# A gated mix of a diagonal state-space layer and linear attention: complex states packed as 64 real and 64 imaginary rows

## The chip, the cores and the metric

The kernel runs on one core of a Trainium2 chip. The core has a matrix engine (PE, TensorE), a vector engine (DVE), an activation engine (ACT, ScalarE), a general engine (POOL, GpSimd) and a queue engine (SP, SyncE). PE reads its operands from the on-chip memory SBUF and writes to PSUM, eight banks of 512 float32 per partition; ACT or DVE must carry a result from PSUM back to SBUF, which is called an evacuation below. Transfers are issued from the queues of SP, ACT and POOL and run on 16 DMA engines. The metric is the device time of one execution in microseconds (us).

## What is computed

```python
g = sigmoid((x * gate_w).sum(-1, keepdims=True))
# a: a diagonal complex recurrence over 2048 steps, 512 states
Lam_bar = exp(dt * Lam);  B_bar = ((Lam_bar - 1) / Lam)[:, None] * (B_re + 1j * B_im)
h[t] = Lam_bar * h[t-1] + B_bar @ x[t]
a = 2 * (h @ C.T).real + x * Dskip
# b: attention without a score matrix, 32 heads of 16
q, k, v = split(x @ wqkv)
phi(u) = concat(softmax(u @ w_phi), softmax(-(u @ w_phi)))
b = (phi(q) @ (phi(k).T @ v)) / (phi(q) @ phi(k).sum(0) + 1e-6) @ wo
out = g * a + (1 - g) * b
```

x has 2048 rows of 512 in bfloat16. The gate g is one number per row.

## The kernel before

The rows of x are taken as 8 residues modulo 8 of 256 steps each, and lie in `xT` transposed, two tiles of 128 rows per residue; there are 16 tiles in all. The recurrence runs over the 256 steps of residue 7 only, with Lam_bar to the eighth, and the other residues follow from it by products with Lam_bar, its square or its fourth power. The 512 states are four groups j of 128.

The program is recorded stage by stage. A stage is a generator, `st_...`, each of whose steps records a few instructions. The table `ORDER` names the steps one after the other; `@` gives the PSUM banks a step takes and `:D` sends its evacuation or scaling to DVE rather than ACT. On every engine the instructions run in that order, each after what it depends on.

- `W`, `T`, `f`: transposes on PE of parts of the weights and of the first two tiles of x, and the product of the key weights with `w_phi`. `Z` are products of zeros ahead of them.
- `k`, `v`, `q`: the key, value and query products of one tile, four matmuls each. `x`, `n`, `e`, `s` (and `X`, `N`, `E`, `S` for queries) are the softmax features: trees of max and min, differences, exponentials and sums, on DVE and ACT, for two or four tiles together. `a` sums phi(k).T @ v in two PSUM banks and, with four matmuls of one column per tile, the gate's sum (L631).
- `V`, `P`, `U`, `M`, `M2`, `D`: from Lambda and dt the factors of the states, by small operations; `D` lays them out as diagonal 128 x 128 matrices `dg` (L437). `i` makes tables of cosines and sines.
- `b`: the product of B with one pair of residues (L641). `g`: the product for the next residue (L653), plus the states before it turned by Lam_bar (L660, L661), then by its square (L668, L669) and fourth power (L674, L675), all summed in PSUM. A complex turn takes, for each of the real and the imaginary result, two matmuls with diagonals. For j 2 and 3 the first turn is made by scalings and accumulating transfers instead (`l`).
- `z`: the scan over 256 steps (L723) with the tables' turns before and after it. `H`, `h`, `p` turn its result into the states of the other residues. They scale by the real part and by the imaginary part on ACT or DVE (L444, L446), and add by DVE (L839 to L843) or by accumulating transfers from POOL's queue (`add_by_dma`, L529). The sets `ZD`, `HD`, `HJ`, `PJ` say for which j a transfer adds.
- `c`: C times the factor of B_bar, in `C2`. `y`: the output products of a tile, eight matmuls with states and C2 (L875) and, for 12 of the 16 tiles, four with the diagonal of Dskip (L882); for the four tiles of `XD` DVE adds the Dskip term (L913, L947). `o`: the attention result (L894) and its normalization. `O`: its transpose by DMA; `t`: the product with `wo` into the same bank as `y` (L943), and the evacuation with the gate. `R` stores.

On SP's queue stand the loads, first the key weights and two tiles of x, then the DMA transposes of x in pairs of tiles (L232), with those of B (L238) and C among them, and from the middle on the transposes of the features and of `on`, and the stores.

Of the kernel before, what the change touches and what calls it, by code (L numbers as in the profile page):

```python
# [10 lines left out]
ALU = mybir.AluOpType  # L11
# [9 lines left out]
P = 128  # L21
# [15 lines left out]
q1@0 H0 z1 v7@1 q1 X0 s3 q7@7 q7 z1 s4 N0 X0 v6@3 b300@0 N0 H0 b301@7 H0:D H0 N0 X0 v6 N0 s3 a2 v5 a2 c0 a2 v7 a2 X0
b301 s3 b300 q4@1 l3:D l3:D l3 c2 X0 N0 H1 H1:D H1:D q4 s4 q5@0 l3 q5 q6@7 g210@6 q6 X1 N1 h0:D H1:D E0 b211@0 X1 s4
E0 b210@7 X1 s3 b210 b311@1 b310@3 g211@2 s4 N1 S0 b211 N1 S0 s4 s4 l3:D X1 g311@7 N1 s4 g210 g210 b310 g211 g211 H1
g310@3 h0 h0 h0 g210 h1:D g211 g210 h1 b311 g211 g210 h0 g211 z2 z2 S0 z2 z2 z2 z2 g311 h1 g311 g311 h1 g310 g310 g310  # L40
S0 p00 v9@2 z2 g310 g310 g311 g311 v8@6 v15@1 S0 z2 z3 v10@7 p00 v12@3 v9 v8 S0 S0 v15 v11@6 z3 z2 z2 H2 v10 q11@2
p00:D z3 z3 z3 H2 a3 a3 H2 v12 z3 H2 H2 v11 h2 p10:D z3 z3 S0 z3 a3 a3 z3 p01 X1 h1 H3 q8@3 H3 H3 q10@6 q10 v14@7 h2
h2 H3 H3 v13@1 v13 p00:D S0 h2 q11 a4 v14 N1 q9@6 h2 q9 h3:D h3:D q12@1 a4 q8 h3 q12 X2 p10 E1 E1 a4 a4 Y S0 h3 h3 Y
X2 G q13@3 q13 G Y Y y1@1 y0@0 y0 N2 END p01 y0 o0@6 p00 p11 o0 S1 o1@4 o1 q15@2 o0 p10 p10 X2 y3@3 S0 y1 p11 S1 o0 X2
N2 q15 o1 S1 o2@6 o2 N2 o2 S1 S1 y3 N2 o1 p01 y3 p10 y2@2 S1 S1 o2 S1 O0 p30 p30 o3@4 o3 o3 y1 y2 X2 y2 q14@6 q14 N2
y6@7 o3 y6 t1 y7@6 G E2 E2 X3 N3 t0 y6 S1 X3 N3 G t0 X3 S1 o4@4 t1 y7 y7 o5@0 o4 o4 N3 O1 t2 X3 p01 N3 S2 S2 S2 o5 o5
t2 o4 S2 o5 S2 t3 t3 y4@4 S2 X3 S1 o6@0 S2 S2 o6 R0 o7@2 p20 y4 y4 o7 N3 p01 o6 o6 p20 o7 o7 y5@5 p30 E3 y5 O2 E3 y5
p20 S2 y8@0 t5 t4 p30:D y11@1 S2 R1 o9@2 p20 p20 p30 y8 t4 t5 o8@4 S3 p11:D p11 S3 S3 o8 S3 y11 o8 o8 o9 o9 o9 O3 t6
# [30 lines left out]
def kernel(  # L79
# [60 lines left out]

    aexp = nc.scalar.activation
# [6 lines left out]
    vec_n = const.tile([12, P], BF16, name="vec_n")  # L148
    vec_m = const.tile([8, P], BF16, name="vec_m")
# [3 lines left out]
    Wk2, Wv = WKV[:, 0, :, 0:DF], WKV[:, 1]  # L153
    C2 = const.tile([P, 2, PT, D], BF16, name="C2")
    warm = const.tile([P, D], BF16, name="warm")
    nc.vector.memset(warm[:], 0.0)
    nc.scalar.dma_start(out=Wc[:], in_=B_w_phi.rearrange("(k hl) e f -> (hl e) k f", hl=8))
# [98 lines left out]
    def xl(n):  # L256
        k = n - XD[0]
        return WKV[:, k // 4, k % 4, :]
# [764 lines left out]
```

## Time and profile before

| | |
|---|---|
| device time, median of 3 runs | 149.28 us (149.17, 149.65, 149.28) |
| the profiled execution | the page gives its span, 147.2 us, and no device time |
| PE busy | 140.8 us, 96% of the span, 1014 matmuls |
| DVE busy | 135.1 us, 92%, 330 instructions |
| ACT busy | 123.4 us, 84%, 222 instructions |
| POOL busy | 45.4 us, 31%, 61 instructions |
| DMA | 22.63 MB; SP's and ACT's queue q1 52.7% and POOL's q0 33.8% of 16 engines' time |

The span runs from the first to the last instruction. A row of a group reads: line, engine, operation, tiles written <- tiles read, shape, count | busy us, mean ns of one | idle time before, and what ended it. A row of waits reads: who waited <- for whom: us in total, times, longest. A row in order of time begins with its start and its length in us. `PS` is PSUM, `C`, `H` and `EE` are tiles whose number is left out. `C` in the first loads is a tile that holds the key weights and two tiles of x before it holds C2.

### The profile page before, as it was taken

To read this page: it belongs to the slowest core of one execution; us is meant where nothing else is said; L and a number is where in the kernel's file an instruction comes from. 1 tells how busy PE (TensorE), PEld (TensorE's weight loads), DVE (VectorE), ACT (ScalarE), POOL (GpSimd) and SP (SyncE) were. 2 spreads that over 40 slices of the span, in tenths; PEclk is the share of its full clock that TensorE was granted. 3 is DMA by queue.
4 is the path that set the end of the run, shared out by engine and by line. 5 is a ranking of instruction groups with operands and counts; after the bars stand their busy time and mean duration, and the time that the engine had idled before them with its cause. 6 is when DMAs were issued, how large, how long until landed. Compare 5 with 4: busy or idle time off the path is not lost.

```text
span 147.2 us, 2881 instructions
## 1 busy us (share of the span) xinstructions
PE 140.8 (96%) x1014; PEld 73.3 (50%) x1014; DVE 135.1 (92%) x330; ACT 123.4 (84%) x222; POOL 45.4 (31%) x61
## 2 busy tenths in 40 slices
PE   6999999999999999999999999999979999999990
PEld 2744444444544644554454656545445554545650
DVE  2879999999999999999999999999998999979740
ACT  3479999999999999999999999999988997912110
POOL 7503600003138195797545353051003003000000
PEclk9999999999999999999999999999999999999999
DMA  5999998990846586789878969969988999999643
GB/s 123 233 184 170 181 179 160 239 290 2 195 94 90 88 114 99 80 127 169 131 111 141 144 90 191 123 126 164 208 179 153 192 214 159 199 180 271 129 111 114
DMA packets 56047, 22.63 MB, mean 154 GB/s; under 512 B 44768, under 2 KB 54880, under 8 KB 56032
## 3 DMA queue, kind: packets, MB, share of 16 engines
q1 hardware_dynamic: 47584, 15.05, 52.7%
q0 software_dynamic: 7504, 7.09, 33.8%
q10 hardware_dynamic: 944, 0.31, 0.9%
q8 instruction: 8, 0.13, 0.4%
q14 instruction: 7, 0.06, 0.1%
HBM read 2.51 MB, written 2.10 MB: 31 GB/s over the span
## 4 chain that ended last, share of the span: by engine, by line
DVE 45%; PE 36%; ACT 9%; DMA 4%; issue 3%; DVEq 0%
PE PS L875 17%; PE PS L943 8%; DVE EE L597 6%; DVE mn L544 5%; DVE mx L544 5%; DMA phT<-EE 4%; DVE EE L555 4%; DVE sq L575 4%; DVE EE L561 3%; PE PS L894 3%; PE PS L493 3%; PE PS L324 2%; DVE w L723 2%; ACT vx L137 2%; ACT Xq L137 2%
## 5 line engine op out<-in xcount | busy, mean ns | idle before, releaser
L567 ACT ACTIVATE EE<-EE 128x2048 bf16<-128x2048 bf16 x16 | 30.3, 1933 | 0.4 <-DVE EE L561 0.4
L493 PE MATMUL PS<-WKV,xT 128*128 128x480 bf16 (+1 forms) x128 | 29.2, 372 | 0.2 <-ACT WKV L137 0.2
L493 PEld LDWEIGHTS <-xT 128*128 128x128 bf16 x192 | 18.1, 97 | 19.7 <-issue 0.9
L137 ACT CAST Xq<-PS 128x480 bf16<-128x480 f32 x32 | 17.5, 592 | 0.2
L653 PE MATMUL PS<-xT,BT 128*128 128x512 bf16 x64 | 16.2, 379 | 0.0
L875 PE MATMUL PS<-C,H 128*128 128x512 bf16 x64 | 15.6, 379 | 0.0
L943 PE MATMUL PS<-Wo,oT 128*128 128x512 bf16 (+2 forms) x68 | 15.5, 366 | 0.0
L493 PE MATMUL PS<-Wq,xT 128*128 128x480 bf16 x64 | 14.9, 365 | 0.0
L641 PE MATMUL PS<-xT,BT 128*128 128x512 bf16 x64 | 14.8, 379 | 0.0
L529 POOL DMA_DIRECT2D C<-CT x4 | 6.8, 1712 | 18.1 <-DVE CT L446 18.1
L907 DVE TENSOR_TENSOR on<-PS,rd 128x512 bf16<-128x512 f32 x16 | 10.9, 684 | 1.0 <-ACT rd L901 0.9
L529 POOL DMA_DIRECT2D eb<-dg x4 | 4.8, 1201 | 22.3 <-ACT dg L444 10.9
L949 ACT ACTIVATE ot<-PS,G 128x512 bf16<-128x512 f32 (+1 forms) x10 | 6.3, 647 | 4.7 <-PE PS L943 4.7
L641 PEld LDWEIGHTS <-BT 128*128 128x128 bf16 x64 | 6.3, 98 | 7.5
L561 DVE TENSOR_TENSOR EE<-mn,Xq 128x2048 bf16<-128x2048 bf16 (+1 forms) x9 | 9.9, 1095 | 0.0
L555 DVE TENSOR_TENSOR EE<-Xq,mx 128x2048 bf16<-128x2048 bf16 (+1 forms) x9 | 9.8, 1094 | 0.0
L575 DVE TENSOR_TENSOR sq<-EE 128x2048 bf16<-128x2048 bf16 (+1 forms) x9 | 9.8, 1094 | 0.0
L943 PEld LDWEIGHTS <-oT 128*128 128x128 bf16 x68 | 6.4, 98 | 6.7
L898 ACT ACTIVATE ld<-PS 128x32 f32<-128x32 f32 x16 | 3.0, 202 | 7.8 <-PE PS L894 7.8
L597 DVE TENSOR_TENSOR EE<-EE,rc 128x2048 bf16<-128x2048 bf16 x8 | 9.6, 1210 | 0.0
L653 PEld LDWEIGHTS <-BT 128*128 128x128 bf16 x64 | 6.1, 97 | 6.9 <-issue 0.2
L137 ACT CAST vx<-PS 128x512 bf16<-128x512 f32 x16 | 9.5, 618 | 0.0
(196 smaller groups left out, 329.7 us busy)
## 6 DMA issues: line engine op xcount, KB each, us to landing
out_dram<-ot SPq DMA_DIRECT2D x7, 256.0 KB, 2.5
C<-CT POOLq DMA_DIRECT2D x4, 256.0 KB, 5.2
eb<-CT POOLq DMA_DIRECT2D x4, 256.0 KB, 4.3
eb<-dg POOLq DMA_DIRECT2D x4, 256.0 KB, 4.3
sq<-sq POOLq DMA_DIRECT2D x3, 256.0 KB, 3.8
WKV<-in_B_wqkv_dram SPq DMA_DIRECT2D x1, 512.0 KB, 4.9
Wo<-in_B_wo_dram SPq DMA_DIRECT2D x1, 512.0 KB, 4.1
WKV<-in_A_x_dram SPq DMA_DIRECT2D x2, 256.0 KB, 4.8
```

The lines of the kernel that those rows point to most:

```text
L137: nc.scalar.copy(out=out_ap, in_=in_ap)
L493: MM(out=pt[:], lhsT=xT[:, kt, ti * P:(ti + 1) * P], rhs=W[:, kt, :], start=(kt == 0), stop=(kt == KT - 1))
L544: VT(out=dst, in0=cur[:, :, :, 0:n, :], in1=cur[:, :, :, n:2 * n, :], op=op)
L555: VT(out=half(EE, 0), in0=X5, in1=live["mx", p].to_broadcast([P, L, 8, Dh, 4]), op=ALU.subtract)
L561: VT(out=half(live["EE", p], 1), in0=live["mn", p].to_broadcast([P, L, 8, Dh, 4]), in1=X5, op=ALU.subtract)
L567: aexp(out=EE[:, l_:l_ + 2], in_=EE[:, l_:l_ + 2], func=ACT.Exp)
L575: VT(out=sq.rearrange("p q x i -> p x q i"), in0=e4[:, :, 0:2], in1=e4[:, :, 2:4], op=ALU.add)
L597: VT(out=E5[:, u:u + 2], in0=E5[:, u:u + 2], in1=rc[:, u:u + 2].to_broadcast([P, 2, 2 * NB, Dh, 4]), op=ALU.mult)
L641: MM(out=pb[:], lhsT=BT[:, ri, kt, j * P:(j + 1) * P], rhs=cells(kt, 2 * pr), start=(kt == 0), stop=(kt == KT - 1))
L653: MM(out=pgq[:], lhsT=BT[:, ri, kt, js], rhs=cells(kt, r1), start=(kt == 0), stop=(dst == 0 and j in LJ and kt == KT - 1))
L875: MM(out=py[:], lhsT=hs[j][ri], rhs=C2[:, 1 - ri, j, c:c + w], start=(j == 0 and ri == 0), stop=False)
L943: MM(out=py[:], lhsT=oT[:, g, :], rhs=Wo[:, g, c:c + w], start=False, stop=(g == HG - 1))
```

## The change

- The states of a group j are packed in another way: 64 states' real parts in partitions 0 to 63 and their imaginary parts in 64 to 127, in two halves q. A turn by a complex factor is then one matmul with a matrix of 2 x 2 blocks of diagonals, in place of two. All factors are made for 8 such groups of 64 (`CT2`), so the small operations have 8 columns, not 4.
- `g` has one matmul where two stood, and for all four j (`l` is gone). `H`, `h` and `p` go through PE too: one matmul per half (`spin4`) and a sum on DVE that reads PSUM; for four of the eight `p`, ACT evacuates and a transfer adds.
- `z` adds the sine product across the halves of the partitions, by two accumulating transfers of 64 partitions each (`swapped`), for all j. The tables are copied into the packed form by eight transfers (`tt`), C by eight (`cc`, into `Cp`).
- B is loaded by rows on SP's queue into `H1` (`Bn`, four loads) and transposed from there.
- The gate is a 481st column among the key weights, padded to 488, so `k` yields it and the 64 matmuls of one column go. `XD` is gone: `Dd` is used for all 16 tiles.
- Tiles of the pools are taken in rotation from fixed buffers (`rotating`), and the whole `ORDER` is another list.

On SP's queue, in the first loads, before (`C_68` is the tile of the key weights and x, `BT` B transposed):

```order
L223 DMA C_68<-in_B_wqkv_dram 128x512 x2
L228 DMA C_68<-in_A_x_dram 128x512 x2
L232 DMA_TRANSPOSE xT<-in_A_x_dram 128x4x256 x5
L238 DMA_TRANSPOSE BT<-in_A_B_re_dram 128x2x512
L232 DMA_TRANSPOSE xT<-in_A_x_dram 128x4x256
```

and now (`H_120` is `H1`):

```order
L240 DMA C_68<-in_B_wqkv_dram 128x512 x2
L245 DMA C_68<-in_A_x_dram 128x512 x2
L255 DMA H_120<-in_A_B_re_dram 64x4x512
L255 DMA H_120<-in_A_B_im_dram 64x4x512
L249 DMA_TRANSPOSE xT<-in_A_x_dram 128x4x256 x4
L261 DMA_TRANSPOSE BT<-H_120 128x8x128 x2
L249 DMA_TRANSPOSE xT<-in_A_x_dram 128x4x256 x2
```

Two loads of B moved ahead of all tiles of x, and the first transposes of B ahead of the fifth pair.

On PE, the turns that follow a product of `g`, before (weights of the diagonals `dg`, the states in `eb` and `H`):

```order
L660 LDWEIGHTS dg
L660 MATMUL PS<-eb_94,dg 128x512
L661 LDWEIGHTS dg
L661 MATMUL PS<-eb_94,dg 128x512
L668 LDWEIGHTS dg
L668 MATMUL PS<-H_117,dg 128x512
L669 LDWEIGHTS dg
L669 MATMUL PS<-H_117,dg 128x512
```

and now, with the last matmul of the product ahead of them:

```order
L691 LDWEIGHTS BT
L691 MATMUL PS<-xT,BT 128x512
L693 LDWEIGHTS dg
L693 MATMUL PS<-eb_98,dg 128x512
L699 LDWEIGHTS dg
L699 MATMUL PS<-H_120,dg 128x512
```

One matmul per turn is left of two. On DVE, where the sums of `H` and `h` stand among the features, before (`m` and `n` are the scaled states, `mx` the features' maxima):

```order
L797 TENSOR_TENSOR H_117<-m_1178,n_1179 128x512
L561 TENSOR_TENSOR EE<-mn,Xq 128x32x64
L799 TENSOR_TENSOR H_117<-m_1178,n_1179 128x512
L446 TENSOR_SCALAR m_1268<-H_116,dgs 128x1024
L446 TENSOR_SCALAR n_1269<-H_116,dgs 128x1024
L795 TENSOR_TENSOR m_1268<-m_1268,H_117 128x1024
```

and now:

```order
L753 TENSOR_TENSOR H_119<-PS,H_119 128x2x256
L586 TENSOR_TENSOR mx_338<-mx_338 128x32x8
L724 TENSOR_TENSOR mc_562<-vv_147,T_144 128x512
L727 TENSOR_TENSOR ms_573<-vv_147,T_144 128x512
L586 TENSOR_TENSOR mx_338<-mx_338 128x32x4
L768 TENSOR_TENSOR H_120<-PS,H_120 128x512 x2
```

The scalings are gone from there, and the sums take one operand from PSUM.

```diff
-B:D Lk Lk Z@0 Lx Z Z Z Z Z Z W00@1 Z B B B W01@2 W01 W01:D W00 W00 W10@0 Lx W11@3 Lx T0@4 B W11 T0 f1@2 Lx Lx f0@1 f0
...
+Z@7 Z Z Z Z Lk Lk W00@3 Z W01@4 W00 W00 Z Lx B:D B B B Lx Z W01 W01:D B T0@5 T0 T1@7 T1 W10@4 W11@1 f1@5 f1 V2@3 Bn Bn
...
+PA = ((0, 0), (0, 1), (1, 0), (1, 1))
-XD = (8, 9, 10, 11)
-LJ = (2, 3)
-ZD = (0, 1)
-HD = (0, 1)
-HJ = (0, 1)
-PJ = (0, 1)
...
+    def rotating(pool, bufs0):
+        slots = {}
+
+        def tile_of(shape, dtype, name, bufs=None):
+            s = slots.setdefault(name, [[], 0])
+            if not s[0]:
+                s[0] = [pool.tile(shape, dtype, name=f"{name}{k}", bufs=1) for k in range(bufs or bufs0)]
+            s[1] += 1
+            return s[0][(s[1] - 1) % len(s[0])]
+
+        return tile_of
...
+    nc.gpsimd.dma_start(out=vec_m[:], in_=gate_w.rearrange("(j p) -> j p", p=P))
     for n, src in enumerate((A_Lambda_im, A_Lambda_re, A_log_dt)):
-        nc.gpsimd.dma_start(out=vec_n[4 * n:4 * n + 4, :], in_=src.rearrange("(j p) -> j p", p=P))
+        nc.gpsimd.dma_start(out=vec_n[CT2 * n:CT2 * (n + 1), :].rearrange("c (d s) -> c d s", d=2),
+                            in_=src.rearrange("(c s) -> c s", s=P // 2).unsqueeze(1).to_broadcast([CT2, 2, P // 2]))
...
+    def st_Bn():
+        for h in range(2):
+            for ri, src in enumerate((A_B_re, A_B_im)):
+                nc.sync.dma_start(out=Bn0[64 * ri:64 * ri + 64, 4 * h:4 * h + 4, :],
+                                    in_=src[2 * h * P:2 * (h + 1) * P, :].rearrange("(c s) d -> s c d", s=64))
+                yield
+
     def st_Lb():
-        for ri, src in enumerate((A_B_re, A_B_im)):
-            for h in range(2):
-                trans(out=BT[:, ri, 2 * h:2 * h + 2, :], in_=src[:, 2 * h * P:2 * (h + 1) * P])
-                yield
+        for j in range(PT):
+            trans(out=BT[:, j].rearrange("p q k m -> p (q k) m"), in_=Bn0[:, 2 * j:2 * j + 2, :].rearrange("p q d -> p (q d)"))
+            yield
...
-            for kt in range(KT):
-                MM(out=live["acc"][1][:, 4 * KVW + ti:4 * KVW + ti + 1], lhsT=xT[:, kt, ti * P:(ti + 1) * P],
-                   rhs=gw_b[:, kt:kt + 1], start=False, stop=(n_ == NTI - 1 and kt == KT - 1), skip_group_check=True)
...
+        MM(out=pgq[:], lhsT=dg[:, 0, c, :], rhs=eb[j][:, q, dst], start=False, stop=(dst == 0))
...
-        MM(out=pgq[:], lhsT=dg[:, da, j, :], rhs=U1[:, 0, :], start=False, stop=False)
-        MM(out=pgq[:], lhsT=dg[:, db, j, :], rhs=U1[:, 1, :], start=False, stop=True)
+        MM(out=pgq[:], lhsT=dg[:, 1, c, :], rhs=U1[:, q, :], start=False, stop=True)
...
+    def swapped(out_ap, in_ap, b):
+        add_by_dma(out_ap[64 * b:64 * b + 64], in_ap[64 - 64 * b:P - 64 * b])
...
+    def spin4(j, k, out_ap, src, t=None):
+        for q in range(2):
+            pb = bank([P, N2], F32, "pb")
+            MM(out=pb[:], lhsT=dg[:, k, 2 * j + q, :], rhs=src[:, q], start=True, stop=True)
+            yield
+            if t is None:
+                VT(out=out_ap[:, q], in0=pb[:], in1=out_ap[:, q], op=ALU.add)
+            else:
+                evac(t[:, q], pb[:])
+            yield
+        if t is not None:
+            add_by_dma(out_ap, t)
+            yield
...
+    def st_cc(h):
+        for q in range(2):
+            for b in range(2):
+                nc.sync.dma_start(out=Cp[64 * b:64 * b + 64, 2 * h:2 * h + 2, q, :], in_=C2[64 * q:64 * q + 64, 1 - b, 2 * h:2 * h + 2, :])
+                yield
...
     def st_h(j):
...
+        yield from spin4(j, 1, H1[:, j], prevs(j))
...
+        yield from spin4(j, 0, eb[j][:, :, pr], src, CT[:, j] if (j, pr) in PA else None)
...
-        for kt in range(KT if n not in XD else 0):
+        for kt in range(KT):
```

More of the change, by code (lines that the diff above doesn't have):

```diff
@@ L262, in st_Ld @@
         yield
-        for n in XD[::2]:
-            k, r = n - XD[0], order[n] // 2
-            w = min(2, len(XD) - k)
-            nc.sync.dma_start(out=WKV[:, k // 4, k % 4:k % 4 + w, :], in_=x_tiles[:, r, 0:w])
-            yield
     def st_Lo():
@@ L327, in st_V @@
     def st_V():
-        pvt = bank([P, 12], BF16, "pvt")
-        nc.tensor.transpose(pvt[:], vec_n[:], ident[0:12, 0:12])
+        pvt = bank([P, 3 * CT2], BF16, "pvt")
+        nc.tensor.transpose(pvt[:], vec_n[:], ident[0:3 * CT2, 0:3 * CT2])
         yield
@@ L713, in st_z @@
         yield
[L714 to L718 removed]
+        for b in range(2):
+            swapped(mc, ms, b)
             yield
[L720 to L723 removed]
+        w = sw([P, 2, NC], BF16, name="w")
@@ L724, in st_z @@
+        for q in range(2):
+            rb = r8_[:, 2 * j + q:2 * j + q + 1].to_broadcast([P, NC])
+            nc.vector.tensor_tensor_scan(out=w[:, q, :], data0=rb, data1=mc[:, q, :], initial=0.0, op0=ALU.mult, op1=ALU.add)
             yield
         hz = H3[:, j, :, ZP:ZP + NC]
-        mc = hz if j in ZD else sw.tile([P, 2, NC], BF16, name="mc")
-        VT(out=mc, in0=w[:], in1=c2, op=ALU.mult)
+        VT(out=hz, in0=w[:], in1=c2, op=ALU.mult)
         yield
-        ms = sw.tile([P, 2, NC], BF16, name="ms")
+        ms = sw([P, 2, NC], BF16, name="ms")
@@ L742, in st_h4 @@
+        for q in range(2):
+            MM(out=ph[:, q, :], lhsT=dg[:, 2, 2 * j + q, :], rhs=H3[:, j, q, ZP - 1:ZP - 1 + NC], start=True, stop=True)
+        yield
         hn = H3[:, j, :, ZP + NC:ZP + N2]
[L743 to L756 removed]
```

415 lines of the change are left out of this document (162 added, 253 removed).

## The prediction

> **What bounds the kernel now.** I read the page's busy shares first, then the table of busy time by stage, then what PE waits for, then PE's rows in order of time. The stage table's columns are the stretch, its length, and busy time of PE, PEld, DVE, ACT and POOL with instruction counts, then PE's granted clock, the DMA share and GB/s.
>
> ```profile
> PE 140.8 (96%) x1014; PEld 73.3 (50%) x1014; DVE 135.1 (92%) x330; ACT 123.4 (84%) x222; POOL 45.4 (31%) x61
> 2.00:4.00 2.00, 2.00 (x6) 0.76 (x5) 0.26 (x5) 1.13 (x1) 1.93 (x6) 1.00 0.99 266
> 20.00:30.00 10.00, 10.00 (x48) 4.58 (x47) 10.00 (x28) 9.99 (x16) 0.00 (x0) 1.00 1.03 206
> 60.00:70.00 10.00, 10.00 (x90) 5.34 (x89) 10.00 (x24) 10.00 (x16) 8.15 (x8) 1.00 0.96 134
> 140.00:147.20 7.20, 3.50 (x24) 1.80 (x21) 2.12 (x3) 1.05 (x2) 0.00 (x0) 1.00 0.38 110
> ...
> DVE 45%; PE 36%; ACT 9%; DMA 4%; issue 3%; DVEq 0%
> ```
>
> The reader is to see three engines full at once in the middle: PE, DVE and ACT each show 10 of 10. The last line is the chain that ended last, by engine. A page like that does not say which of them a change must relieve. Modelled ends can also make PE look full when it is not, so I check PE's pitch, the distance from one matmul's start to the next.
>
> ```profile
> PE PS L324 <- DVE warm L156: 1.2, 1, 1.2
> PE PS L894 <- DMA phT<-EE: 1.1, 1, 1.1
> PE PS L493 <- ACT WKV L137: 0.2, 1, 0.2
> ...
> L493 PE MATMUL PS<-Wq,xT 128*128 128x480 bf16 x64 | 14.9, 365 | 0.0
> L641 PE MATMUL PS<-xT,BT 128*128 128x512 bf16 x64 | 14.8, 379 | 0.0
> ...
> 22.16 3.62 PE L641 MATMUL PS<-xT,BT 128*128 128x512 bf16 x16
> ...
> 90.33 0.24 PE L631 MATMUL PS<-gw_b,xT 128*128 128x1 bf16 x4
> 90.43 0.41 PE L627 MATMUL PS<-vx,EE 128*128 128x68 bf16 x8
> ...
> 91.14 0.97 PE L493 MATMUL PS<-Wq,xT 128*128 128x480 bf16 x4
> ...
> 99.23 0.39 PE L882 MATMUL PS<-Dd,xT 128*128 128x128 bf16 x4
> 99.46 1.03 PE L875 MATMUL PS<-C,H 128*128 128x512 bf16 x4
> ```
>
> A run of one line lasts (count - 1) pitches and one modelled duration (the mean ns of its group). A 512-wide matmul has a pitch of (3.62 - 0.38) / 15 = 0.216 us, a 480-wide one (0.97 - 0.37) / 3 = 0.200. Four 128-wide ones take 0.23 until the next begins, 0.057 each; four gate matmuls take 0.10, 0.025 each. The 48 matmuls of 20 to 30 us at 0.216 make 10.4 us. So PE is not merely shown busy, it issues wide matmuls back to back and is the bound of the whole middle. Its idle time is the 1.2 us at the start, 0.2 and 1.1 us of waits, and the 3.7 us of the end (7.2 - 3.5): 6.2 of the 6.4 us that its busy time leaves of the span. The page times one execution at a span of 147.2 us. The median of the runs is 149.28, so 2.1 us lie around the span; I carry them unchanged.
>
> The Trainium skill (TensorE: Matmul & The Clock Gate, Back-to-back issue gap) puts a sustained stream of weight loads and matmuls at about 131 ns for N=512 and 81 ns for N=128. These rows show 216 and 57, so the trace disagrees with both; by the page the eight wide and sixteen narrow matmuls counted below would cost 2.3 us in place of 2.6, an estimate from its figures.
>
> **PE's work, part by part.** One product per complex factor halves the rotations in L660 to L675 from 24, 16 and 16 matmuls to 16, 8 and 8: sixteen fewer 512-wide and eight fewer 256-wide, with the first rotation now on PE for j 2 and 3 too. But the rotations that DVE and ACT did as scalings now go through PE: `H` adds 8 of 256, `h` adds 8 and `p` adds 16 of 512. Net: 512-wide 48 where 40 stood, 256-wide 16 as before. That is 8 x 0.216 = +1.73 us. Without `XD` every one of the 16 output tiles multiplies by `Dd`: 16 x 0.057 = +0.91. The gate column rides in the k products, so 64 gate matmuls go: 64 x 0.025 = -1.60. The 64 k matmuls are 8 columns wider; between the 480 and 512 rows a column costs 0.0005 us, +0.26 in all. PE has 1.3 us more to do, in the stage where nothing covers it.
>
> **What the other engines lose.** Of scalings and sums:
>
> ```profile
> L444 ACT ACTIVATE CT<-H,dgs 128x1024 bf16<-128x1024 bf16 x7 | 8.1, 1156 | 0.0
> L444 ACT ACTIVATE dg<-H,dgs 128x512 bf16<-128x512 bf16 x5 | 3.5, 710 | 0.0
> L137 ACT CAST H<-PS 128x512 bf16<-128x512 f32 x8 | 4.7, 626 | 0.0
> L907 DVE TENSOR_TENSOR on<-PS,rd 128x512 bf16<-128x512 f32 x16 | 10.9, 684 | 1.0 <-ACT rd L901 0.9
> L841 DVE TENSOR_TENSOR Bn<-CT,dg 128x512 bf16<-128x512 bf16 x4 | 1.6, 414 | 0.0
> L947 DVE SCALAR_TENSOR_TENSOR ot<-PS,G,xd 128x512 bf16<-128x512 f32 x4 | 3.0, 748 | 0.2
> ```
>
> ACT loses 11 scalings of 1024 and 14 of 512 and gains 8 evacuations of 512: 11 x 1.16 + 14 x 0.71 - 8 x 0.63 = 17.7 us less. DVE gains 20 sums with one operand in PSUM. No such sum with a bf16 partner is in the trace: L841 (no PSUM, 0.41) and L947 (0.75) bound it, and I take L907's 0.68, the same operation from PSUM: +13.7. It loses 14 sums of 512 and the 8 instructions of `XD`, 14 x 0.41 + 8 x 0.75 = 11.7, and some thirty scalings and sums more; at L841's 0.41 each (an estimate) another 12, so about 10 us net. On the sum these reliefs count for nothing, because PE covers both engines; they count only in the waits that PE had on them. The wait on phT (1.1) ends when DVE and ACT finish a group's features, so I let all of it go: -1.1, between 0 and -1.3 (the 0.2 before L493 with it). Should the cover fail, it is late features again that PE would see, at o and t.
>
> **The start.** B now comes in rows and is transposed from SBUF, with two 256 KB loads put on SP's queue ahead of all tiles of x.
>
> ```profile
> xT<-in_A_x_dram SPq DMA_TRANSPOSE x7, 4.2
> ...
> C<-in_A_x_dram SPq DMA_DIRECT2D x2, 128.0 KB, 3.9
> ...
> 1.72 0.90 SPq L228 DMA_DIRECT2D C<-in_A_x_dram  x2
> 2.66 7.36 SPq L232 DMA_TRANSPOSE xT<-in_A_x_dram  x5
> ...
> 1.25 3.17 PE L324 MATMUL PS<-warm 128*128 128x512 bf16 x7 [1.25 <-DVE warm L156]
> 5.97 0.39 PE L316 MATMUL PS<-ident,C 128*128 128x128 bf16 x4
> 7.80 0.97 PE L493 MATMUL PS<-WKV,xT 128*128 128x480 bf16 x4 [0.20 <-ACT WKV L137]
> ...
> 36.29 0.90 SPq L266 DMA_DIRECT2D WKV<-in_A_x_dram  x2
> 85.48 10.01 SPq L613 DMA_TRANSPOSE phT<-EE  x2
> ...
> 2.82 0.52 POOL L164 DMA_DIRECT2D vec_n<-in_A_log_dt_dram  x1
> ...
> vec_n<-in_A_log_dt_dram POOLq DMA_DIRECT2D x1, 1.0 KB, 3.8
> ```
>
> The DMA engines are full then (0.99 at 266 GB/s), so 512 KB delay the tiles by 2.0 us: the first lands at about 2.66 + 4.2 + 2.0 = 8.9, each next 1.47 later (7.36 / 5). PE's new order needs tile 2 after eight matmuls of k1 and k0, at some 9.8, tile 7 at 12.2 against a landing of 11.8, and B at 16.3 against 14.8: covered everywhere, with as little as 0.4 us. Ahead of that PE now puts the transposes of x (landing 1.72 + 3.9 = 5.6 and later) before those of W10 and W11, and the vector transpose before f2, with vec_n behind one more issue on POOL (2.82 + 0.52 + 3.8 = 7.1). I read k's start at 8.15 in place of 7.80: +0.35, between 0 and +3 (every tile of x late by more than its slack). SP later carries eight copies of C and four transposes of B in place of loads; its queue issues nothing from 37.2 to 85.5 us now (36.29 + 0.90, then 85.48), so I cost them at nothing, and if that cover went, phT's transposes behind them would be late.
>
> **The middle and the end.** `z` now swaps halves by accumulating DMA for all four j, where j 2 and 3 used DVE. Between a swap and its use on DVE the new order keeps at least 4.2 us of other DVE work (j = 0, my count by rows such as those above).
>
> ```profile
> mc<-ms POOLq DMA_DIRECT2D x4, 64.0 KB, 3.0
> ...
> 43.05 1.73 POOL L529 DMA_DIRECT2D mc<-ms  x2 [2.29 <-DVE ms L712]
> ...
> 143.31 0.62 DVE L951 TENSOR_SCALAR ot<-PS,G 128x384 bf16<-128x384 f32 x1 [0.99 <-PE PS L943]
> 143.54 0.37 ACT L949 ACTIVATE ot<-PS,G 128x128 bf16<-128x128 f32 x1 [0.19 <-PE PS L943]
> ```
>
> A pair costs 0.87 of issue and 3.0 to land, 3.9 us: covered, by 0.3 us. For such waits, and for banks that free late, I add +0.3 (0 to +2). At the end the last product is the whole tile 14, not the narrow half of tile 15: its evacuation on DVE is L951's kind at 512 wide, between 0.62 and 0.75 (L947), in place of one that was over 0.4 us after PE. +0.2, between 0 and +0.4.
>
> **Sum.** +1.3 +0.35 -1.1 +0.3 +0.2 = +1.05 us on the span of 147.2: 148.2, and 150.3 with what lies around it. With every term at its lower end this case gives 149.3; with the start at 0.7, the new waits at 1.0, the end at 0.4 and phT's wait half gone it gives 152.1.
>
> **Rivals.**
> First, faster: PE, DVE and ACT are all full, and PE's own gaps are due to them. For it: the last-ending chain puts 45% on DVE. Against it: PE's pitch. All that lighter engines can give back are PE's gaps, 1.3 us of waits and, with a better start and end, perhaps 0.7 more, against 1.3 more work: 147.2 + 1.3 - 2.0 = 146.5, some 148.6 by the runs. It decides once more than 1.75 us of gaps come back. The Trainium skill (Perfetto Trace Analysis, Identifying the Most-Contended Engine) would support it: matmul busy share is no measure of closeness to the limit, the share of weight loads is, and here that is 50%. The trace bears that out only where matmuls are narrow; with 512-wide ones the pitch decides.
> Second, the tiles of x or B come late: if the two loads cost the 4.8 us that a 256 KB load takes to land (the row of WKV below) and not 2.0, PE waits 2.4 us more before tile 7: 152.7.
>
> ```profile
> WKV<-in_A_x_dram SPq DMA_DIRECT2D x2, 256.0 KB, 4.8
> ```
>
> Third, a swap or a copy of C lands late before the outputs: one landing not covered, 3.0 us less what cover there is, about +1.5: 151.8. The same holds where phT's wait merely moves.
> Fourth, PE's slow start lasts longer.
>
> ```profile
> L324 PE MATMUL PS<-warm 128*128 128x512 bf16 x8 | 3.8, 631 | 1.2 <-DVE warm L156 1.2
> ```
>
> The seven first matmuls have a pitch of (3.17 - 0.63) / 6 = 0.42, twice the later one; five of them now stand ahead of the first transposes. If PE's gaps before 6 us keep it slow to 8 us, about 2 us of work double: 152.3. The Trainium skill (TensorE: Matmul & The Clock Gate, Part 1: The HAM clock gate) says a clock gate doubles the rate after some 3.4 us of sustained activity; the rows agree with such a step between 4.4 and 6 us, though the granted clock reads 1.00 throughout.
>
> **Chances.** The forecast 0.60, of which 0.15 falls within 0.3% (0.45 us, about what this kernel's measurement can tell from no change); the faster rival 0.13, with 0.02 of it in that band; late tiles 0.14; late swaps 0.09; the slow start 0.04. So faster 0.11, same 0.17, slower 0.72. The range that leaves out 2 in 10 runs from 148.9, inside the first rival, to 152.7, the second rival's time.
>
> **What would show it.** Right: PE full from 20 to 140 us with a 512-wide pitch of 0.216; its busy time up by 1 to 1.5 us while DVE falls to about 125 and ACT to about 106; no wait of PE on phT above 0.5; k products starting near 8.15. Wrong: the row of PE waits names xT, BT, H or C with more than 1 us, or PE's gap at the end shrinks below 3.5. The forecast falls if PE's busy time does not rise.

## The result, and the profile after

The changed kernel takes 158.0 us, median of four runs from 156.4 to 159.2, against 149.2 before: a ratio of 1.056, 95% interval 1.049 to 1.063. The forecast was 150.3, with a range up to 152.7: the direction was right, the size wrong by 7.7 us. The ratio leaves out the slowest of the four runs (159.2; without it the median is 157.4), whose profile is the one after, with a span of 157.5 and a mean clock of 0.972; the other three, at 0.975 to 0.989, are below 1 too.

The page's busy shares, the slices of PE, DVE and PE's clock, then the stage table of 10 us, and what PE and DVE waited for:

```profile
PE 144.7 (92%) x974; PEld 74.0 (47%) x974; DVE 128.9 (82%) x298; ACT 110.9 (70%) x206; POOL 42.4 (27%) x62
...
PE   6799999996269999999999999998999999999990
...
DVE  2679999902979999998999999999999998646421
...
PEclk9999999999956999999999999999999999999997
...
30.00:40.00 10.00, 7.86 (x38) 3.53 (x36) 3.17 (x12) 4.79 (x12) 0.00 (x0) 1.00 1.10 146
40.00:50.00 10.00, 6.29 (x21) 2.54 (x21) 9.01 (x18) 8.39 (x16) 2.33 (x3) 0.66 0.45 75
150.00:157.50 7.50, 3.47 (x26) 1.84 (x24) 1.85 (x3) 1.27 (x2) 0.00 (x0) 0.87 0.30 87
...
PE PS L704 <- ACT H L131: 3.2, 1, 3.2
PE PS L532 <- ACT Xq L131: 2.6, 1, 2.6
...
PE PS L849 <- DVE mx L586: 0.6, 1, 0.6
...
DVE T L472 <- DMA T<-phT: 6.8, 2, 6.6
```

DVE and ACT are lighter, by 6.2 and 12.5 us where about 10 and 17.7 were forecast, and PE is full after 50 us as before but for the wait of 0.6. Most of the loss stands in one hole, between 30 and 50 us: DVE stops first, then ACT, then PE. In order of time:

```profile
23.97 4.76 POOL L506 DMA_DIRECT2D T<-phT  x8 [3.49 <-ACT phT L150]
...
31.37 0.29 DVE L625 TENSOR_TENSOR sq<-sq 128x256 bf16<-128x256 bf16 x1
...
38.23 0.42 DVE L472 TENSOR_SCALAR T<-T 64x1024 bf16<-64x1024 bf16 x1 [6.56 <-DMA T<-phT]
...
39.01 0.31 ACT L632 ACTIVATE lg<-smf 128x128 f32<-128x128 f32 x1 [5.21 <-DVE smf L628]
...
40.49 1.02 PE L532 MATMUL PS<-WKV,xT 128*128 128x512 bf16 x4 [2.63 <-ACT Xq L131]
...
44.73 0.37 PE L704 MATMUL PS<-H,dg 128*128 128x256 bf16 x1 [3.22 <-ACT H L131]
...
T<-phT POOLq DMA_DIRECT2D x8, 128.0 KB, 11.2
```

POOL issues the eight copies of the cosine and sine tables (`tt`) at 24 us. They take 11.2 us to land, where the swaps of half their size, 64 KB, take 3.0. DVE's in-order queue stands at the scaling of the cosine by -1 (L472). Behind it stand the features' sums; ACT's queue stands at a logarithm of such a sum; behind that stand the evacuations, and PE has no bank.

### The profile page after: what moved, and what is told of

Same layout as the page of the kernel before. It is cut to its first block, busy times and chain, and to the rows that moved or that the text cites. A ratio compares the mean times of both kernels' runs of the same rounds, so it can differ in the third digit from the quotient of the medians.

```text
span 157.5 us, 2774 instructions
## 1 busy us (share of the span) xinstructions
PE 144.7 (92%) x974; PEld 74.0 (47%) x974; DVE 128.9 (82%) x298; ACT 110.9 (70%) x206; POOL 42.4 (27%) x62
## 4 chain that ended last, share of the span: by engine, by line
PE 43%; DVE 29%; DMA 10%; ACT 6%; issue 5%; POOL 5%; POOLq 0%; DVEq 0%; ACTq 0%
PE PS L831 15%; PE PS L532 9%; PE PS L890 9%; DMA T<-phT 7%; DVE mx L586 3%; DVE mn L586 3%; DMA mc<-ms 3%; PE PS L849 3%; PE PS L765 3%; DVE w L735 2%; POOL T L506 2%; PE PS L838 2%; DVE EE L603 2%; DVE EE L639 2%; DVE EE L597 2%
## 5 line engine op out<-in xcount | busy, mean ns | idle before, releaser
L532 PE MATMUL PS<-WKV,xT 128*128 128x512 bf16 (+1 forms) x128 | 32.3, 396 | 2.6 <-ACT Xq L131 2.6
L532 PEld LDWEIGHTS <-xT 128*128 128x128 bf16 x192 | 19.1, 101 | 27.3 <-issue 9.4
L131 ACT CAST Xq<-PS 128x488 bf16<-128x488 f32 (+1 forms) x32 | 17.2, 576 | 0.4 <-PE PS L532 0.3
L831 PE MATMUL PS<-Cp,H 128*128 128x512 bf16 x64 | 15.8, 379 | 0.0
L862 DVE TENSOR_TENSOR on<-PS,rd 128x512 bf16<-128x512 f32 x16 | 10.8, 687 | 3.3 <-ACT rd L856 3.2
L896 ACT ACTIVATE ot<-PS,G 128x512 bf16<-128x512 f32 (+1 forms) x11 | 7.2, 673 | 7.6 <-PE PS L890 7.6
L568 POOL DMA_DIRECT2D mc<-ms x8 | 7.0, 1046 | 20.2 <-DVE ms L727 17.3
L568 POOL DMA_DIRECT2D H<-ms x8 | 7.8, 1159 | 14.0 <-DVE ms L741 13.2
L853 ACT ACTIVATE ld<-PS 128x32 f32<-128x32 f32 x16 | 3.1, 192 | 11.2 <-PE PS L849 11.1
L568 POOL DMA_DIRECT2D eb<-CT x4 | 5.6, 1398 | 18.3 <-ACT CT L131 18.3
L898 DVE TENSOR_SCALAR ot<-PS,G 128x512 bf16<-128x512 f32 (+1 forms) x6 | 4.1, 683 | 7.2 <-PE PS L890 7.1
L691 PEld LDWEIGHTS <-BT 128*128 128x128 bf16 x64 | 6.1, 98 | 7.1
## 6 DMA issues: line engine op xcount, KB each, us to landing
T<-phT POOLq DMA_DIRECT2D x8, 128.0 KB, 11.2
```

Of the source, the lines that this page charges most:

```text
L131: nc.scalar.copy(out=out_ap, in_=in_ap)
L532: MM(out=pt[:], lhsT=xT[:, kt, ti * P:(ti + 1) * P], rhs=W[:, kt, :], start=(kt == 0), stop=(kt == KT - 1))
L568: nc.gpsimd.dma_start(out=out_ap, in_=in_ap, accum_op=ALU.add)
L691: MM(out=pgq[:], lhsT=BT[:, j, q, kt, :], rhs=cells(kt, r1), start=(kt == 0), stop=False)
L831: MM(out=py[:], lhsT=hs[j][ri], rhs=Cp[:, j, ri, c:c + w], start=(j == 0 and ri == 0), stop=False)
L862: VT(out=live["on", g_][:, u], in0=pn[:, :, :, 0:Dh], in1=rd[:].unsqueeze(3).to_broadcast([P, 2, 16, Dh]), op=ALU.mult)
```

## The experiments

**The table copies.** Theory A: the late copies make the hole. Theory B: all transfers are late there, and PE would wait for another. First the copies were issued sooner, with half of them moved to where they are used:

```diff
-... i0 i3 i0 i3 ... M2 g100 ... v3@1 tt0 c1:D n2 s0 tt0 tt1 tt1 ... tt0:D tt1 s0 tt1 v1@0 tt1:D ... x3 H1@2 ... h0@1 z2
+... i0 i1 i0 i1 ... M2 tt0 tt0 tt0 tt0 g100 ... v3@1 c1:D n2 s0 ... tt0:D s0 v1@0 ... x3 tt1 tt1 tt1 tt1 H1@2 ... h0@1 tt1:D z2
```

> The table for states j = 1 is made before that for j = 3, so the first four table copies are issued at about 20.5 us and not at 24.0; the other four are issued only behind the swaps of z1, and their scaling on DVE stands just ahead of z2. All else, PE's order too, is as in the changed kernel. Theory A (DVE stands 6.6 us at the scaling of a table that lands late, and evacuations and PE stop behind it): the wait of DVE on the tables falls below 1 us, PE's two waits of 2.6 and 3.2 us near 40 us go, its granted clock stays at 1.00, and the time falls from 158.0 to 150.5 (149.8 to 151.5). Theory B (all transfers of 25 to 45 us are late since the DMA engines are full, and PE would wait for another of them): 155 or more, with PE's wait on another tile.

152.7 us (152.5 to 153.1), 1.024 of before (1.021 to 1.027). The copies land in 3.9 us, DVE's wait for the tables and PE's two waits near 40 us are gone, the clock is 1.00:

```profile
PE 142.1 (94%) x974; PEld 73.1 (48%) x974; DVE 128.8 (85%) x298; ACT 110.7 (73%) x206; POOL 42.5 (28%) x62
...
30.00:40.00 10.00, 10.00 (x50) 4.65 (x48) 8.69 (x22) 9.97 (x21) 1.75 (x2) 1.00 0.79 135
40.00:50.00 10.00, 8.63 (x82) 5.03 (x81) 9.97 (x22) 9.21 (x17) 7.04 (x9) 1.00 0.45 78
...
PE PS L668 <- DVE EE L639: 1.4, 1, 1.4
...
T<-phT POOLq DMA_DIRECT2D x8, 128.0 KB, 3.9
```

So the late copies are worth 5.3 of the 8.8 us (4.7, counted from 157.4). Theory A holds for them, but 2.2 us more than it gave are left, and a new wait shows at `a1` (L668). Leaving the copies out altogether:

```diff
-                nc.gpsimd.dma_start(out=T2[64 * b:64 * b + 64, q, ...], in_=T2n[64 * q:64 * q + 64, ...])
-        c2, s2 = T2[:, :, 0, j], T2[:, :, 1, j]
+        c2, s2 = (T2n[:, a, j].unsqueeze(1).to_broadcast([P, 2, NC]) for a in range(2))
```

> The eight table copies are left out; z reads the uncopied tables, so both halves of the partitions turn by a wrong table in most states, and the scaling by -1 works on half as many elements. Theory A: no wait of DVE on the tables, no hole of PE near 40 us, 150.2 (149.5 to 151). Theory B: with 1 MB less to move other transfers land sooner too, so the time falls as well, but PE keeps a wait over 1 us near 40 us: 152 to 155.

153.1 us, no better than copies that land in time: once covered, the copies cost nothing.

**Why they are late.** Is it POOL's queue, the bytes queued, or what runs beside them?

```diff
-                nc.gpsimd.dma_start(out=T2[...
+                nc.scalar.dma_start(out=T2[...
```

> The eight table copies are issued from ACT's queue and not from POOL's, at the same places of the list. If POOL's queue makes them late (Theory A1): they land 3 to 5 us after issue, as other loads do, DVE's wait shrinks to 1 us or less, 151 (150 to 152.5, ACT has 4 us of issues more). If the 16 DMA engines are full and any queue waits for its share (Theory A2): they land 8 us or more after issue, DVE still waits over 4 us, 156 to 160.

166.3 us. Neither reading came out as written. ACT issues its first copy only at 31 us, behind its other work, and its own queue then stops at the issues, the last three of which take 5.5 us:

```profile
T<-phT ACTq DMA_DIRECT2D x8, 128.0 KB, 5.1
...
37.20 5.53 ACTq L506 DMA_DIRECT2D T<-phT  x3
```

From issue to landing is short because the wait now stands ahead of the issue. On ACT's queue the kernel is slower; since the copies start 7 us later there, the run does not say how they would do on another queue at the old time. Next, half the bytes at the old time:

```diff
-... tt0 tt1 tt1 ... tt1 v1@0 tt1:D ... x3 H1@2 ... z2
+... tt0 ... v1@0 ... x3 tt1 tt1 tt1 tt1 H1@2 ... tt1:D z2
```

> The changed kernel with four of the eight table copies (those of j = 2 and 3) and their scaling moved to their later use; the first four are issued at 24.0 us as in the changed kernel. If what counts is how much the DMA engines have queued at 24 to 32 us (0.5 MB less of it now): the four land in 5 us or less of their issue, DVE waits under 1 us, 152.7 to 153.3, as with the early tables. If what counts is the time of issue: they land after 8 us or more, DVE waits 2 us or more, 154.5 to 157.

157.1 us; the four copies issued at 24 us took up to 11.3 us, and DVE still waited 5.5. It is not their own number. Then what runs beside them: one of C's transposes as a plain load of the same 256 KB, and, in another run, a pause on SP's queue while the copies run.

```diff
+                if (h, ri) == (1, 1):
+                    nc.sync.dma_start(out=CT[:, 2 * h:2 * h + 2, ri, :], in_=src[2 * h * P:2 * (h + 1) * P, :].rearrange("(j p) d -> p j d", p=P))
```

> The changed kernel with its late tables, in which one of C's four transposes, the one issued at 24.86 us beside the table copies, is replaced by a plain load of the same 256 KB (its half of C is then not transposed, so the output is of another C). If the copies crawl because transposes run beside them (the engines moved 72 to 118 GB/s at 30 to 34 us, while 300 at 26 to 28): they land within 7 us, DVE waits 2.5 us or less, 153.5 to 155.5. If the bytes queued ahead of them count: still 9 us or more to land, over 4.5 us of waits, 156 to 159.

156.4 us: between the two readings, 8.0 us to land and a wait of 3.4. For the pause, the issues on SP's queue come in another order (a list of the issues, not code):

```diff
-(SP) Lv, Bn (4th), Lc (4th), Lb (3rd), Lq
+(SP) Bn (4th), Lb (3rd), Lv, Lc (4th), Lq
```

> The changed kernel with its eight table copies at 24.0 us, and on SP's queue alone another order: the last load of B and the third transpose of B, which waits for it, ahead of the load of the value weights and the last transpose of C. So SP issues nothing for some 4 us while the copies run. If other transfers on the engines make the copies late: they land within 7 us, DVE waits under 2 us, 153 to 154.5. If it is the time of their issue or POOL's queue alone: they land after 9 us or more, DVE waits over 4 us, 156.5 to 159.

The time does not tell: the four runs lie between 154.5 and 159.4, and the value weights, now issued later, make PE wait 4.1 us. Neither reading came out whole: the copies land in 4.0 us in the median, but the last of them take up to 8.5, and DVE waits 4.2 us for these. What tells is the stage table. In rows of 2 us, the last two columns being the share of the 16 DMA engines and GB/s, first the changed kernel:

```profile
28.00:30.00 2.00, 2.00 (x12) 0.98 (x10) 2.00 (x3) 2.00 (x4) 0.94 (x3) 1.00 1.27 195
30.00:32.00 2.00, 2.00 (x12) 0.94 (x10) 1.67 (x7) 2.00 (x5) 0.00 (x0) 1.00 1.11 72
32.00:34.00 2.00, 2.00 (x11) 0.92 (x10) 0.00 (x0) 1.80 (x4) 0.00 (x0) 1.00 1.20 118
```

with the plain load:

```profile
30.00:32.00 2.00, 2.00 (x12) 0.95 (x10) 1.65 (x7) 2.00 (x5) 0.00 (x0) 1.00 1.12 243
```

and with the pause on SP's queue, whose next issue after 24.2 us is a transpose of B at 27.45:

```profile
27.45 1.95 SPq L261 DMA_TRANSPOSE BT<-H  x1
...
28.00:30.00 2.00, 2.00 (x12) 0.99 (x11) 2.00 (x3) 2.00 (x4) 0.93 (x3) 1.00 0.96 221
30.00:32.00 2.00, 2.00 (x12) 0.95 (x10) 1.64 (x7) 2.00 (x5) 0.00 (x0) 1.00 1.19 105
...
T<-phT POOLq DMA_DIRECT2D x8, 128.0 KB, 4.0
```

Full engines move 221 GB/s with the copies all but alone and 243 beside a plain load, but 72 to 118 in the stretches where they share with transposes. With the pause the copies are issued at the same 24 us from the same queue, and most of them are through before that transpose runs. So it is the company on the DMA engines that makes them late, not their queue, their number or their time.

The company acts in two ways. POOL's queue q0, which carries the copies, moved this much from 26 to 28 us (packets, MB, share of the 16 engines), first in the changed kernel, then with the pause:

```profile
q0 software_dynamic: 41, 0.12, 15.8%
```

```profile
q0 software_dynamic: 136, 0.40, 88.5%
```

In the changed kernel q1 holds 78.8% there and moves 0.50 MB at a good rate (310 GB/s by both queues): the copies first stand behind loads that SP issued just ahead of them, the value weights above all. Only then, from 28 us on, comes the slow mixture. By the medians the copies take 4.0 us with the pause, 8.0 with the value weights and a plain load of C beside them, and 11.2 with the transpose of C in place of that load: about 4 us for the transfers beside them and about 3 for the transposing.

It is not every company of a transpose: with the early tables copies and a transpose of C share the stretch from 24 to 26 us, and the engines move 275 GB/s:

```profile
24.00:26.00 2.00, 2.00 (x11) 0.91 (x10) 2.00 (x5) 1.99 (x4) 0.00 (x0) 1.00 1.13 275
```

What makes the one mixture slow and not the other, no run shows.

**The clock.** Products of zeros fill PE's holes while DVE still waits:

```diff
+        for _ in range({3: 12, 1: 13}.get(ti, 0)):
+            MM(out=pv[:], lhsT=warm[:, 0:P], rhs=warm[:], start=False, stop=False, skip_group_check=True)
```

> The changed kernel with its late tables, and products of zeros of 512 columns in both holes of PE: 12 behind v3 and 13 behind v1, added into the banks of v3 and v1, so that none of them waits for what PE waits for there. Theory C (the halved clock costs time of its own): clock 1.00 throughout and 2 us or more less than the changed kernel, 155.5 to 156. Theory D (the time is set by DVE's stall and its features, which come late whether PE runs fast or slow after the hole): 157 to 159, no change that can be told, with PE waiting at a0 or a1 for DVE instead.

159.0 us, as Theory D has it. In the changed kernel the clock falls to half behind the hole (first row, 6 matmuls in 2 us). With the filler it stays at 1.00 (second fence, 12 matmuls), and PE waits 1.1 us for DVE's EE at `a1` (third).

```profile
46.00:48.00 2.00, 2.00 (x6) 0.76 (x5) 2.00 (x5) 2.00 (x6) 0.00 (x0) 0.50 0.00 0
```

```profile
44.00:46.00 2.00, 2.00 (x12) 1.01 (x11) 2.00 (x5) 2.00 (x6) 0.00 (x0) 1.00 0.00 0
```

```profile
48.43 0.68 PE L670 MATMUL PS<-vx,EE 128*128 128x68 bf16 x16 [1.10 <-DVE EE L641]
```

The slow clock costs next to nothing there, because DVE's features come no sooner. In the changed kernel DVE starts the last step of `a1`'s EE 10.8 us after it starts to scale the first table (38.23 and 49.04 us), and has EE ready at 50.26; PE, at its slow clock, comes to `a1` at about 50.4. With the filler the same two starts are 11.4 us apart (35.78 and 47.16). The tables landed 2.4 us sooner in this profiled run, which the edit does not account for, and PE is 2.0 us ahead of the changed kernel's profile at 50 us; it loses that again behind a late swap (DVE waits 1.8 us for it at 89 us, PE 1.5 for ACT's vx at 92) and at phT (1.2 us). A first filler, half of which ended up waiting for the same evacuation as PE, had given 159.9 and told nothing:

> Products of zeros, added into banks that are in use, fill PE's two holes near 40 us: 12 of 512 columns behind v3 and 26 of 256 ahead of the third turn of g011, 5.4 us of PE's time in 5.8 us of waits. DVE still waits for the tables. If the fall of the granted clock to 0.5 after the holes costs time of its own (Theory C): clock 1.00 throughout, the some 20 matmuls after 44.7 us at 0.2 us and not 0.41, 2.3 us less than the changed kernel: 155.7 (155 to 156.5). If the holes alone cost (Theory D): 158, no change, or some tenths more.

**The start.** The changed kernel starts its k products at 9.20 us, not at 8.15. With the early tables, W10 and W11 were put back ahead of x's tiles:

```diff
-... W01 W01:D B T0@5 T0 T1@7 T1 W10@4 W11@1 f1@5 ...
+... W01 W01:D B W10@4 W11@1 T0@5 T0 T1@7 T1 f1@5 ...
```

> The kernel with the early tables, and the transposes of W10 and W11 put back ahead of those of the two tiles of x, as in the kernel before. Theory E (k starts at 9.20 us since W10 and W11, and with them the key weights, stand on PE behind two waits for x's landing): k starts near 8.2 us and the time falls by 1.0, from 152.7 to 151.7 (151.3 to 152.2). Theory F (the two loads of B delay x's tiles, which k needs too): k's start stays above 8.8 us, 152.3 or more.

154.9 us, slower by 2.2. PE's rows of that start (taken from the run that also moves `a1`) show why: W10's bank waits for W01's evacuation, which DVE makes at 6.8 us behind the products BD, and BD waits for the identity from POOL, which is 0.7 us later than before since POOL issues one more load first. The tiles of x had only filled that gap; without them PE idles, and its slow clock lasts to 12 us and beyond.

```profile
6.79 0.42 DVE L133 COPY Xq<-PS 128x512 bf16<-128x512 bf16 x1
7.27 0.61 PE L322 MATMUL PS<-ident,C 128*128 128x128 bf16 x8 [1.46 <-DVE Xq L133]
...
10.40 2.86 PE L532 MATMUL PS<-WKV,xT 128*128 128x488 bf16 x7
```

With the group's mean of 0.58 in these rows, (2.86 - 0.58) / 6 is a pitch of 0.38, not 0.20, and the granted clock of 10 to 12 us reads 0.50. The 40 k products take 9.65 us there, and 8.39 with the early tables. So the identity was made sooner, W01 went to ACT, and other banks were taken:

```diff
-    nc.gpsimd.dma_start(out=vec_m[:], ...)
+    nc.scalar.dma_start(out=vec_m[:], ...)
-... W01 W01:D B T0@5 T0 T1@7 T1 W10@4 W11@1 f1@5 f1 V2@3 ... f0@0 ... V@1 ...
+... W01 W01 W10@2 W11@1 T0@5 B T0 f1@4 ... f0@3 f0 W10:D f1:D V2@0 V2 T1@6 T1:D W11 ... k0@3 f2@5 f2 f3@4 k1@2 f3:D V@1 ...
```

> The kernel with the early tables, and another start: the gate weights are loaded from ACT's queue, so that POOL makes the identity 0.7 us sooner; W01 is evacuated by ACT and not by DVE behind the small products BD; W10 and W11 take other banks and stand ahead of the tiles of x, f1 and f0 between these. Theory I (k starts late because W01 waits for DVE, which waits for POOL's identity): PE has no gap over 0.5 us between 5.3 and 7.5 us, k starts near 8.0, and the time falls by 1.2, from 152.7 to 151.5 (151.1 to 152.0). Theory F (the tiles of x are late behind the loads of B): k's second or third tile waits for xT, 152.3 or more. If a gap of PE keeps its clock at half until 11 us or later, as in the last start tried: 154 or more.

153.7 us: k starts at 8.06 as meant, and 1.1 us earlier is already lost at 22 us, with waits of 0.3 to 0.4 on ACT's evacuations. The vectors' transpose (V) had slipped to 9.4 us; put ahead again:

```diff
-... V2@0 V2 T1@6 T1:D W11 ... k1@2 f3:D V@1 V Lb P P P2 P2 U ...
+... V2@0 V2 V@7 V T1@6 T1:D W11 P P P2 P2 ... k1@2 f3:D Lb U ...
```

> The second start, with the transpose of the vectors and the factors' first steps put back ahead (on PE behind f0, on ACT and DVE ahead of f2's and f3's evacuations). If the second start lost its 1.1 us because the factors, and with them the tables and the diagonals, came 0.9 us later (Theory J): no wait of PE for ACT at 17 to 25 us, 1.0 less than the early tables alone, 151.7 (151.2 to 152.2). If ACT's evacuations bound PE there (Theory K): waits of PE on eb, H or Xq stay, 152.5 to 153.7.

153.6 us. The waits at 17 to 25 us are gone but for one of 0.24 and PE is 0.3 to 0.5 us ahead at 20 to 29 us, so Theory J is right about the place; but at `a1` PE waits 1.6 us instead of 1.4, and the gain is gone.

**What holds a1.** `a1` was put later on PE, with the first other start, and with the second together with H1:

```diff
-... a0@45 a0 v2 s1 a1 a1 z1 ... k12 w2@6 x3 n3 x3 tt1 tt1 tt1 tt1 H1@2 s2 w2 k14@3 k14 ...
+... a0@45 a0 v2 s1 z1 ... k12 a1 a1 w2@6 x3 n3 x3 tt1 tt1 tt1 tt1 s2 w2 k14@3 H1@2 k14 ...
```

> As the run with the start mended, and a1, which waited 1.4 us for DVE's features after the table wait was gone, stands some 2 us later on PE, behind two further products. If that wait is only a place in the list: it goes, 1.4 us less than the run before, 150.3 (149.9 to 151.0). If DVE is behind for good there: another wait of PE takes its place within 10 us, less than 0.5 us is gained.

> As the run with the second start, with a1 some 2 us later on PE and the first product of H1 one product later, which waited 1.4 and 0.9 us. Both waits are places in the list: 0.9 less than the run before, 150.6 (150.1 to 151.2). If DVE is behind for good there: less than 0.4 us gained.

155.1 and 153.2 us, within 0.5 of the starts that they were tried on. The wait at `a1` is gone. In the first, PE waits 0.9 us for H1's swap instead, at 48 us; in the second, with H1 later too, the same 0.9 stands at the swap of H0, at 56 us. Next DVE's scaling of C, which waits 1.2 us for ACT, went behind the features:

```diff
-... v0 c3 c0:D n3 x3 ... a0 v2 s1 a1 a1 z1
+... v0 c3 n3 x3 ... a0 v2 s1 a1 a1 c0:D z1
```

> The kernel with the early tables, and DVE's scaling of C for j = 0, at which DVE waited 1.2 us for ACT, behind the features of a1. If that wait is what makes a1's features late (Theory L): PE's wait of 1.4 us at a1 falls below 0.4, and the time falls by 1.0, from 152.7 to 151.7 (151.3 to 152.2). If the features wait for ACT's exponentials or the scan all the same (Theory M): less than 0.4 us gained.

152.7 us, no gain: DVE reaches the scan sooner and now waits there for the swap, and PE waits longer at `a1`.

```profile
PE PS L668 <- DVE EE L639: 2.0, 1, 2.0
...
DVE w L735 <- DMA mc<-ms: 2.8, 2, 2.2
```

Both edits together:

> Both edits together, the third start and the later scaling of C. If Theories J and L hold and both gaps were PE's own: 150.7 (150.2 to 151.3). If only one holds: about 151.7. If PE is held there by DVE and ACT, so that what is gained at one place is lost at the next: 152.2 or more.

151.7 us (151.1 to 152.0 in three runs, 153.4 in one), 1.016 of before (1.012 to 1.021): some 1.0 less, the best version found, and slower than before all the same. The number is that of "only one holds", but each edit alone had gained nothing; why the two together do is not shown. With `a1` and H1 later too it is 152.8, no better:

> As the run with the third start and C's later scaling (151.7), and a1's products some 2 us and H1's first product one product later on PE, as tried once before. If the wait at a1 is now only a place in the list: 1.0 less, 150.7 (150.2 to 151.2). If it moves to H1 or the next product that needs DVE: 151.3 or more.

**Is PE the bound at the end?** From the best version the Dskip products of four tiles are left out:

```diff
-        for kt in range(KT):
+        for kt in range(KT if n not in (8, 9, 10, 11) else 0):
```

> As the run with the third start and C's later scaling (151.7), with the 16 products of 128 columns by Dskip's diagonal left out for four of the 16 output tiles (so the Dskip term is missing in those rows) and nothing put in their place. If PE is the bound in the last third: 16 x 0.057 = 0.9 us less, 150.8 (150.3 to 151.3). If another engine or a transfer bounds there: 151.4 or more.

152.5 us: nothing gained. The 0.9 us are there, and stand as waits for the features' and the attention result's transposes, where the profile of the best version has no wait of PE after 104 us:

```profile
134.62 0.68 PE L849 MATMUL PS<-KVm,phq 128*128 128x68 bf16 x16 [0.79 <-DMA phq<-EE]
135.50 1.04 PE L890 MATMUL PS<-Wo,oT 128*128 128x512 bf16 x4 [0.20 <-DMA oT<-on]
```

The same four tiles with the Dskip term on DVE, as the kernel before has it, had been tried on the version with the second start and the later `a1`:

```diff
+                nc.vector.scalar_tensor_tensor(out=ot, in0=py[:], scalar=G[:, ti:ti + 1], in1=live["xd", n][:, c:c + w], op0=ALU.mult, op1=ALU.add)
```

> As the run before, with the Dskip term of four output tiles on DVE again, as in the kernel before (loads of x, a product, and the sum in the evacuation): 16 matmuls of 128 columns less on PE. If PE is the bound in the last third and nothing covers its work: 16 x 0.057 = 0.9 us less, 149.7 (149.2 to 150.3). If waits on DVE and the transposes set that stage: within 0.3 us of the run before, or slower.

154.6 us, 1.4 more than without, with 1.1 us of waits for `oT` and 0.6 for phq that the version without has not. What PE is spared there is lost behind DVE and the transposes.

## Why the prediction was wrong

- **PE's work, +1.3: right.** Matmul counts times the pitches of the prediction give 137.7 us against 136.5, and PE's busy time at full clock is 142.1 against 140.8.
- **New waits, +0.3 (0 to +2): the step that failed.** It counted the swaps of `z` and late banks. The eight table copies stood in the account of the change but were given no price and no cover, nor was DVE's scaling behind them. The stretch from 30 to 50 us lost 8.2 us of PE's time by the pitches: 5.8 in two waits, the rest by the halved clock. With the copies issued sooner the time fell by 5.3 us, and without them by 4.9. The third rival had the kind of wait right, a copy that lands late; but it looked ahead of the outputs, named C's copies, and gave 1.5 us.
- **The price of such a copy** would have come out wrong, too: the row of the swaps gives 3.0 us, the copies take 3.9 at best in the median, and 11.2 in the company that they had. The DMA share of 1.03 at 20 to 30 us stood in a quoted row, and only that of the start (0.99) was read. The Trainium skill (Advanced Engine Details and Errata, X-Bar Transpose (TRN2)) says that transposes are as fast as other transfers; the rows of 72 to 118 GB/s at full engines, against 243 with the same 256 KB as a plain load, disagree for some mixtures of transposes and copies, the row of 275 does not.
- **"PE covers both engines, the reliefs count for nothing": wrong in reach.** PE's pitch showed that it was never starved before, not by how much. At `a1` and at the last features DVE and the transposes are within about 1 us of PE, as the runs show in which a gain of PE (1.1 us at the start, 0.9 at the end) turned into a wait.
- **The reliefs themselves, about -10 on DVE and -17.7 on ACT:** measured -6.2 and -12.5. The price of a sum from PSUM was right (0.68 to 0.69 us); what made the rest smaller was not worked out. These terms do not enter the sum.
- **The start, +0.35: measured +1.4**, within its bounds, but not by the tiles of x. The transposed ones came in time (40 k products without a gap, so the second rival did not happen), and PE's waits of 0.6 us for the first two tiles lie ahead of 7.27 us, when W10 can start in either order. The step looked at SP's queue; the late operand came through POOL's, by way of the identity, BD and W01. That an earlier start alone does not win it back is due to what stands close behind PE at `a1`.
- **phT's wait, -1.1: about half.** 0.6 remain. **The end, +0.2: right**, 7.50 - 3.47 = 4.0 us against 3.7.
- **The fourth rival**, a slow clock that lasts: not at the changed kernel's start, but behind the hole, where it cost next to nothing, and in the start that was tried first, where the 40 k products took 1.3 us more. The faster rival did not happen: PE's gaps grew.

In the profile the terms add up: 1.2 + 1.4 + 8.2 - 0.5 + 0.3 = 10.6, against 157.5 - 147.2 = 10.3. That the direction came out as forecast is mostly luck: the forecast rested on PE's work, which is 1.2 of these. The profile with early tables has a span of 151.1, still 3.9 above 147.2. Its records place 1.2 in PE's work, about 1.2 in the start, 1.4 at `a1`, 0.4 in a wait for vx at 86 us and 0.3 at the end, with 0.4 back at phT; that these are not independent is shown, how they divide is not.

## What to carry to other kernels

List every transfer that a change adds, with who waits for it and what stands behind that waiter in its queue; a wait for a transfer at the head of a full in-order engine stops all that this engine serves. Price a transfer by a row with the same company on the DMA engines, those queued just ahead of it included, and if it is late, move it away from that company; another queue did not help here. An engine without gaps is a bound only as far as its next rival is behind; take a little work off it before counting its work one for one.

## What the hardware showed that was not expected

- Copies and transposes together moved as little as 72 GB/s with all engines full, and in another stretch 275.
- One of four runs of the first other start took 304.5 us, the other three 154.2 to 155.0. PE ran at half speed from end to end, 24 matmuls of 512 columns or so in 10 us where 48 is usual, and the granted clock read 1.00 throughout:

```profile
PE 296.0 (98%) x974; PEld 117.1 (39%) x974; DVE 131.9 (44%) x298; ACT 115.5 (38%) x206; POOL 40.0 (13%) x62
...
20.00:30.00 10.00, 10.00 (x24) 3.36 (x23) 7.62 (x26) 5.04 (x11) 4.42 (x12) 1.00 1.20 200
```

The Trainium skill (TensorE: Matmul & The Clock Gate, Seeing it yourself) warns that the events of this gate are unreliable in traces and that it has been seen stuck at a quarter of the clock for over 50 us; this run is of that kind, at half the usual pace for 300 us. Here the pitch tells PE's speed, and the granted clock does not.
